# A list scheduler's urgency taken from a backward pass in which every engine does one operation at a time

## The chip, the core and the metric

One core of a Trainium2 chip runs the whole program. The metric is the time of one execution on the device in microseconds (us), the median of three runs. The core has the engines TensorE (PE in the profile), VectorE (DVE), ScalarE (ACT) and GpSimd (POOL); SyncE (SP) issues most of the transfers, ScalarE some.

## The reference

A retention block (attention with a decay in place of the softmax) is followed by a two-layer network with a PReLU between:

```python
# q, k, v: (8, 8, 576, 64) float32
scores = scale * np.matmul(q, k.transpose(0, 1, 3, 2))          # scale = 1/8
gamma = 1.0 - 2.0 ** (-5.0 - np.arange(H))                      # one decay per head
Dmat = np.where(rel >= 0, gamma[:, None, None] ** rel, 0.0)     # rel = row - column
attn = np.matmul(scores * Dmat, v)
x = attn.transpose(0, 2, 1, 3).reshape(4608, 512)
h = x @ w_in                                                    # (512, 2048), float64 input
g = np.maximum(h, 0.0) + alpha * np.minimum(h, 0.0)             # alpha: (2048,)
out = (g @ w_out).astype(np.float32)                            # (2048, 512), float64 input
```

## The kernel before

The sequence of 576 tokens is worked in chunks of 64. A "pair" is two heads of one batch; there are 32 pairs. A "joint" of a pair computes scores inside the chunks, and the state that is carried from chunk to chunk; the masked scores and the states go through small transfers into `at` and `vn`, and the "values" of the pair are computed from them in the next joint. Their results land in tiles `x` of 256 tokens, 18 in all, which the network consumes.

The network's products are made of reduced-precision pieces (`fp32r`) that together keep float32's accuracy: an operand is split into three pieces, and each unit does three products. The first units are done with plain float32 operands instead, while the weights are still being converted (from float64 words, on ACT, DVE and POOL) and split.

Every operation is first recorded in `ops` in program order, with its engine, a cost, and its dependencies (by tile and key), and only then put in order by `plan()` and emitted:

```python
def do(eng, cost, fn, r=(), w=(), late=0.0, lock=False):   # records one operation
    ...
def dma(to, fro, size, r, w, eng="SP"):
    queue = {"SP": nc.sync, "ACT": nc.scalar}[eng]
    do(eng, 0.56, lambda: queue.dma_start(to(), fro()), r, w, late=size / RATE)
```

The operations that are spoken of below, with the line that the profile gives them (cuts marked with "..."):

```python
# L629, L631 (ACT), L639, L641, L650 (DVE), L653 (POOL): one piece of a weight, from float64 words to float32
def convert(raw, wa, to, c=None): ...
# L677 (ACT), L678 (POOL), L681 (DVE): a float32 weight into three pieces
def split_w(at, room_=None): ...

# a pair's operands
def operands(n):
    ...
    do("POOL", 1.15, f, (), four, lock=True)                    # L719: q scaled, qx <- qx, tabx
    ...                                                         # L726: transposes on DVE
    do("ACT", 0.7, f, (), [(kn, 0), (kn, 1)])                   # L731: k scaled, kn <- kn, tabk

def values(n, pv):
    ...  nc.tensor.matmul(pv[i]..., vns[n % 2][:, h2, j], mt.get()[:, h2, j], ...)    # L747, into psh
    ...  nc.scalar.copy(g.get()[:, c, o * C:(o + m) * C], pv[i]...)                   # L762, x <- psh

def joint(n):
    pv = [Gen(psh[m]) for m in range(2)]
    ...  values(n - 1, pv)
    ...                                                         # L785: last chunk's scores, into psh
    ...                                                         # L793: scores, into psa
    ...                                                         # L802: states of the chunks, into psa
    # L816 (ACT) and L822 (POOL), or L831 (DVE): masks; L838 (DVE): the last chunk's
    # L844, L854 (ACT), L849, L857, L860 (DVE): prefix states su, from psa; then stored and loaded as vn

def split_x(vis):        # L906, L918 (ACT), L920, L923 (POOL): x into its three pieces lx
def unit_plain(cell):    # L940 (PE, psh), L946 (ACT), L951 (DVE): first layer, plain
def second_plain(cell):  # L970 (PE, pso): second layer, plain
def unit(cell):          # L1004 (PE, psh), L1012, L1016 (ACT), L1013, L1019 (DVE)
def split_g(cell):       # L1028, L1030 (ACT), L1032, L1035 (POOL)
def second(cell):        # L1053 (PE, pso); L1071, L1076 (DVE): the sums leave PSUM
```

`plan()` is a list scheduler. It walks forward in time; at each step it takes, for every engine, the operations whose dependencies are met, and among those that can start within a small slack of the earliest it picks the one with the smallest `due`. How `due` is made is what changes:

```python
at = 0.0
want = [1e9] * len(ops)
for op in ops:
    if op.eng == "PE":
        want[op.n] = at
        at += op.cost
best = None
for turn in range(TURNS):                    # TURNS = 1
    due = [1e9] * len(ops)
    for op in reversed(ops):
        due[op.n] = min([want[op.n]] + [due[u.n] - wait(op, u) - op.cost - op.late
                                        for u in users[op.n]])
    ...                                      # the forward pass
    while len(order) < len(ops):
        for e, queue in ready.items():
            ...
            c = [(earliest(op), op) for op in queue
                 if e != "PE" or op.n <= rest[0] + AHEAD_PE]
            t0 = min(t for t, _ in c)
            t, op = min((x for x in c if x[0] <= t0 + SLACK.get(e, 0.05)),
                        key=lambda x: (due[x[1].n], x[1].n))
```

Each engine then runs its operations in the order in which they are emitted.

Of the kernel before, what the change touches and what calls it, by code (L numbers as in the profile page):

```python
# [21 lines left out]
def kernel(  # L22
# [95 lines left out]
    for i in range(NBIT - 1):  # L118
# [8 lines left out]
                            op=ALU.mult)  # L127
# [37 lines left out]
    ops = []  # L165
# [56 lines left out]
    LAT = {"PE": 0.2}  # L222

    def plan():

        users = [[] for _ in ops]
        for op in ops:
            for d in op.deps:
                users[d.n].append(op)

        def wait(d, op):
            return 2.0 if d.late else 0.0 if d.eng == op.eng else LAT.get(d.eng, 0.1)

        at = 0.0
        want = [1e9] * len(ops)
        for op in ops:
            if op.eng == "PE":
                want[op.n] = at
                at += op.cost
        best = None  # L240
        for turn in range(TURNS):
            due = [1e9] * len(ops)
            for op in reversed(ops):
                due[op.n] = min([want[op.n]] + [due[u.n] - wait(op, u) - op.cost - op.late
                                                for u in users[op.n]])
            left = [len(op.deps) for op in ops]
            ready = {e: [] for e in BEGIN}
            rest = [op.n for op in ops if op.eng == "PE"]
            end, begin, order = [0.0] * len(ops), [0.0] * len(ops), []
            free, held, port, wire = dict(BEGIN), {}, [0.0, ""], 0.0  # L250
            can = [0.0] * len(ops)
            for op in ops:
                if not op.deps:
                    ready[op.eng].append(op)

            def earliest(op):
                t = max(free[op.eng], can[op.n])
                for b in op.banks:
                    if b in held:
                        t = max(t, max([x + LAT.get(e, 0.1) for e, x in held[b].items()  # L260
                                        if e != op.eng] or [0.0]))
                if op.lock and port[1] != op.eng:
                    t = max(t, port[0])
                if op.late:
                    t = max(t, wire - BACKLOG)
                return t

            while len(order) < len(ops):
                pick = None
                for e, queue in ready.items():  # L270
                    if not queue:
                        continue
                    c = [(earliest(op), op) for op in queue
                         if e != "PE" or op.n <= rest[0] + AHEAD_PE]
                    if not c:
                        continue
                    t0 = min(t for t, _ in c)
                    t, op = min((x for x in c if x[0] <= t0 + SLACK.get(e, 0.05)),
                                key=lambda x: (due[x[1].n], x[1].n))
                    if pick is None or t < pick[0]:  # L280
                        pick = t, op
                t, op = pick
                ready[op.eng].remove(op)
                if op.eng == "PE":
                    rest.remove(op.n)
                begin[op.n] = t
                free[op.eng] = t + op.cost
                end[op.n] = t + op.cost
                if op.late:
                    wire = max(wire, t + op.cost) + op.late  # L290
                    end[op.n] = wire
                for b in op.banks:
                    held.setdefault(b, {})[op.eng] = t + op.cost
                if op.lock:
                    if port[1] == op.eng or t + op.cost > port[0]:
                        port[:] = [t + op.cost, op.eng]
                order.append(op)
                for u in users[op.n]:
                    left[u.n] -= 1
                    can[u.n] = max(can[u.n], end[op.n] + wait(op, u))  # L300
                    if not left[u.n]:
                        ready[u.eng].append(u)
            total = max(end)
            if best is None or total < best[0]:
                best = total, order, begin[:], end[:]
            for op in ops:
                if op.eng == "PE":
                    want[op.n] = 0.5 * want[op.n] + 0.5 * (begin[op.n] - GAIN * (op.n / len(ops)))
        return best

    TURNS, AHEAD_PE, GAIN = 1, 150, 0.0
    BACKLOG = 2.0
    LAG, FIRST = 2, range(4, 8)
    SLACK = {"PE": 0.02}
    BEGIN = {"PE": 5.0, "ACT": 0.5, "DVE": 8.2, "POOL": 5.8, "SP": 0.5}
# [553 lines left out]
    order = [(0, (0, 1)), (1, (0, 1, 2, 3)), (0, (2, 3))]  # L869
# [310 lines left out]
    at = 8  # L1180
# [19 lines left out]
    for cell in cells[8:]:  # L1200
# [6 lines left out]
        for _ in range(late.get(n, 0)):  # L1207
            at = nlate[0]
# [14 lines left out]
    for cell in pend:  # L1223
        second(cell)
    best = plan()
    for op in best[1]:
        op.fn()
# [31 lines left out]
```

## Time and profile before

| | |
|---|---|
| median of 3 runs | 987.82 us (987.67 to 990.02) |
| span of the profiled execution | 988.3 us |
| instructions | 22,760 |
| mean granted TensorE clock | 0.981 of full speed |
| transfers | 134.93 MB, 137 GB/s over the span |
| DMA share of the 16 engines, first 25 us and next 25 us | 1.10 and 1.02 |

The profile is of one execution. Busy time is given for each engine, with the number of instructions; a row of 40 digits shows the busy share in each fortieth of the span (24.7 us), in tenths. The time that is asked about is the time of the last instruction, so what counts is the chain of work that ends there, and the idle time of the engine that carries that chain. A wait is put down to what released it: "PE psh L785 <- ACT x L762" is idle time of PE before line 785 which ended when line 762 on ACT was done. A group shown as "x8" in a timeline is eight instructions drawn together.

### The profile page before, as it was taken

The numbers are of one execution on the slowest core, as the hardware profiler recorded it, in microseconds if no ns is written. First come the engines' busy times: TensorE is split into PE (matmuls) and PEld (weight loads), VectorE is DVE, ScalarE is ACT, GpSimd is POOL, SyncE is SP. The second block draws the span as 40 slices with busy tenths as digits, with TensorE's granted clock in tenths as the row PEclk, the third lists the DMA queues.
The fourth block names the chain that finished last, engine by engine and source line by source line (L and its number), as shares of the span: only waits on it lengthen the run. The fifth ranks groups of instructions, "written<-read, shape, count | busy, mean of one in ns | idle before, by whom it ended". The sixth has DMA issues, their size and how long they took to land.

```text
span 988.3 us, 22760 instructions
## 1 busy us (share of the span) xinstructions
PE 942.5 (95%) x8713; PEld 825.2 (83%) x8713; DVE 614.6 (62%) x1294; ACT 582.9 (59%) x1313; POOL 636.1 (64%) x515
## 2 busy tenths in 40 slices
PE   4897889999999999998999999999999999999998
PEld 4664568898888888887888899999999999999996
DVE  5767766778566777785656777564455444544444
ACT  3564455757566757574677766665555555555542
POOL 3757655666766758575596999675655556566543
PEclk9797989999999999999999999999999999999999
DMA  9969688788665978778442545243222221221111
GB/s 240 211 135 228 145 201 177 184 177 200 171 135 145 209 157 215 169 202 184 152 160 97 162 147 161 74 143 105 64 64 75 71 92 64 65 75 54 43 44 64
DMA packets 255052, 134.93 MB, mean 137 GB/s; under 512 B 218448, under 2 KB 218464, under 8 KB 254944
## 3 DMA queue, kind: packets, MB, share of 16 engines
q1 hardware_dynamic: 238624, 130.59, 51.1%
q10 hardware_dynamic: 16320, 2.89, 2.0%
q8 instruction: 68, 1.11, 0.5%
q14 instruction: 40, 0.33, 0.1%
HBM read 82.19 MB, written 35.65 MB: 119 GB/s over the span
## 4 chain that ended last, share of the span: by engine, by line
PE 82%; DMA 5%; SPq 3%; issue 3%; DVE 2%; POOL 2%; ACT 2%; ACTq 0%; POOLq 0%; DVEq 0%
PE psh L1004 36%; PE pso L1053 35%; PE psh L747 3%; SPq L220 3%; DMA kn<-in_k_dram 2%; PE psh L940 2%; PE pso L970 1%; PE psa L793 1%; PE psa L802 1%; DMA qx<-in_q_dram 1%; DMA w<-in_q_dram 1%; DMA w<-in_moe_w_out_dram 1%; PE psh L785 1%; DMA vn<-in_v_dram 0%; POOL lx L923 0%
## 5 line engine op out<-in xcount | busy, mean ns | idle before, releaser
L1004 PEld LDWEIGHTS psh<-lx,w 128*128 128x128 f32 x3264 | 411.3, 192 | 15.8 <-DVE ga L1019 2.5
L1004 PE MATMUL psh<-lx,w 128*128 128x256 f32 x3264 | 420.5, 285 | 2.3 <-DVE ga L1019 0.9
L1053 PE MATMUL pso<-w,g 128*128 128x512 f32 x1632 | 403.1, 394 | 1.1 <-POOL g L1035 0.7
L1053 PEld LDWEIGHTS pso<-w,g 128*128 128x128 f32 x1632 | 296.9, 189 | 58.9 <-POOL g L1035 1.7
L1032 POOL TENSOR_TENSOR g<-ga,g 128x512 fp32r<-128x512 f32 x136 | 179.2, 1318 | 254.2 <-ACT g L1028 253.9
L1013 DVE SCALAR_TENSOR_TENSOR ga<-psh,gt 128x256 f32<-128x256 f32 x272 | 114.4, 421 | 185.0 <-ACT gt L1012 179.7
L1035 POOL TENSOR_TENSOR g<-g 128x512 fp32r<-128x512 f32 x136 | 177.4, 1304 | 11.6 <-ACT g L1030 1.4
L1019 DVE SCALAR_TENSOR_TENSOR ga<-psh,malpha,ga 128x256 f32<-128x256 f32 x272 | 130.6, 481 | 69.9 <-ACT psh L1016 68.0
L1016 ACT ACTIVATE psh<-ga 128x256 f32<-128x256 f32 x272 | 105.2, 388 | 92.5 <-DVE ga L1013 91.7
L1028 ACT ACTIVATE g<-ga 128x512 fp32r<-128x512 f32 x136 | 85.8, 631 | 116.9 <-PE pso L1053 98.1
L1012 ACT COPY gt<-psh 128x256 f32<-128x256 f32 x272 | 100.9, 371 | 58.2 <-PE psh L1004 50.3
L923 POOL TENSOR_TENSOR lx<-lx 128x512 fp32r<-128x512 f32 x78 | 100.9, 1308 | 17.5 <-DVE lx L913 16.9
L1030 ACT ACTIVATE g<-ga 128x512 fp32r<-128x512 f32 x136 | 84.4, 620 | 0.0
L831 DVE SCALAR_TENSOR_TENSOR at<-psa,pf,mask 64x256 f32<-64x256 f32 x96 | 46.4, 483 | 17.1 <-PE psh L747 9.5
L906 ACT ACTIVATE lx<-x 128x512 fp32r<-128x512 f32 x78 | 47.2, 627 | 0.0
L719 POOL TENSOR_TENSOR qx<-qx,tabx 128x576 f32<-128x576 f32 x28 | 32.6, 1165 | 21.6 <-DMA qx<-in_q_dram 10.4
L747 PEld LDWEIGHTS psh<-at,vn 128*64 128x64 f32 x1008 | 32.9, 137 | 12.9 <-issue 7.6
L920 POOL TENSOR_TENSOR lx<-x,lx 128x512 fp32r<-128x512 f32 x30 | 38.5, 1299 | 3.8 <-ACT lx L918 3.8
L747 PE MATMUL psh<-at,vn 128*64 128x64 f32 x1008 | 38.1, 226 | 2.3 <-DVE ga L1019 2.1
L1071 DVE TENSOR_TENSOR op<-pso,op 128x512 f32<-128x512 f32 x46 | 31.5, 685 | 13.7 <-PE pso L1053 13.7
L731 ACT ACTIVATE kn<-kn,tabk 128x576 f32<-128x576 f32 x28 | 21.7, 776 | 24.4 <-DMA kn<-in_k_dram 22.4
L762 ACT COPY x<-psh 128x256 f32<-128x256 f32 (+3 forms) x84 | 23.8, 320 | 18.7 <-PE psh L747 9.5
(173 smaller groups left out, 868.3 us busy)
## 6 DMA issues: line engine op xcount, KB each, us to landing
ok<-o SPq DMA_DIRECT2D x48, 256.0 KB, 3.4
op<-ok SPq DMA_DIRECT2D x24, 512.0 KB, 4.0
x<-xk SPq DMA_DIRECT2D x23, 512.0 KB, 3.6
xk<-x SPq DMA_DIRECT2D x18, 512.0 KB, 4.2
out_dram<-o SPq DMA_DIRECT2D x36, 256.0 KB, 4.1
kx<-in_k_dram SPq DMA_DIRECT2D x112, 72.0 KB, 3.3
vn<-in_v_dram SPq DMA_DIRECT2D x56, 144.0 KB, 3.5
at<-qT SPq DMA_DIRECT2D x56, 144.0 KB, 3.4
```

What stands on the lines that cost most here:

```text
L747: nc.tensor.matmul(pv[i].get()[half(h2), (j - js[0]) * C:(j - js[0] + 1) * C], vns[n % 2][:, h2, j], mt.get()[:, h2, j], start=True, stop= ...
L923: do("POOL", 1.29, lambda c=c: nc.gpsimd.tensor_tensor(out=piece(to.get()[:, 2, c]), in0=to.get()[:, 0, c], in1=to.get()[:, 1, c], op=ALU. ...
L1004: nc.tensor.matmul(at(b), piece(w[:, l, c0:c0 + P]), piece(x.get()[:, l, cc]), start=(n == 0 and cc == 0), stop=(n > 0 and cc == NCC - 1), ...
L1012: do("ACT", 0.36, lambda t=t, at=at: nc.scalar.copy(t(), at(1)), [(ph, 1)], [(gt, f)])
L1013: do("DVE", 0.42, lambda t=t, g=g, at=at: nc.vector.scalar_tensor_tensor(out=g(), in0=at(0), scalar=ONE, in1=t(), op0=ALU.mult, op1=ALU.su ...
L1016: do("ACT", 0.39, lambda g=g, at=at: nc.scalar.activation(at(1), g(), ACTF.Relu, scale=-1.0), [(ga, f)], [(ph, 1)])
L1019: do("DVE", 0.48, lambda g=g, at=at, fc=fc: nc.vector.scalar_tensor_tensor(out=g(), in0=at(1), scalar=malpha[:, fc:fc + 1], in1=g(), op0=A ...
L1028: do("ACT", 0.64, lambda: nc.scalar.mul(piece(to.get()[:, 2]), ga.get(), BELOW), both, [(to, 2)])
L1030: do("ACT", 0.64, lambda: nc.scalar.mul(piece(to.get()[:, 0]), ga.get(), BELOW * 2.0 ** -12), both, [(to, 0)])
L1032: do("POOL", 1.29, lambda: nc.gpsimd.tensor_tensor(out=piece(to.get()[:, 1]), in0=ga.get(), in1=to.get()[:, 2], op=ALU.subtract), both + [ ...
L1035: do("POOL", 1.29, lambda: nc.gpsimd.tensor_tensor(out=piece(to.get()[:, 2]), in0=to.get()[:, 0], in1=to.get()[:, 1], op=ALU.subtract), [( ...
L1053: nc.tensor.matmul(a[2 * m + b].get(), piece(g.get()[:, l, f, m * P:(m + 1) * P]), piece(w_at[u, 2 + f].get()[:, l]), start=(cell["first"] ...
```

## The change

The order of the operations is to follow better what each engine can do. Before, an operation's urgency was the latest start at which PE could still keep its program order, found along the dependencies alone: many operations of one engine may then be due at once, and the list does not tell which of them has to begin early so that all are done. Now a list scheduler first runs backwards, from the last operation to the first: every engine does one operation at a time, the operation latest in the program goes first, and the time to the end that it finds, negated, is `due`. The loop over `TURNS`, which ran once, is taken out, and with it `want` and `GAIN`. The forward pass, with its costs and constants, is the same:

```diff
-        at = 0.0
-        want = [1e9] * len(ops)
-        for op in ops:
-            if op.eng == "PE":
-                want[op.n] = at
-                at += op.cost
-        best = None
-        for turn in range(TURNS):
-            due = [1e9] * len(ops)
-            for op in reversed(ops):
-                due[op.n] = min([want[op.n]] + [due[u.n] - wait(op, u) - op.cost - op.late
-                                                for u in users[op.n]])
+        due = [0.0] * len(ops)
+        left = [len(users[op.n]) for op in ops]
+        can = [0.0] * len(ops)
+        free = {e: 0.0 for e in BEGIN}
+        ready = {e: [] for e in BEGIN}
+        for op in ops:
+            if not left[op.n]:
+                ready[op.eng].append(op)
+        for _ in ops:
+            pick = None
+            for e, queue in ready.items():
+                if queue:
+                    t0 = min(max(free[e], can[op.n]) for op in queue)
+                    op = max((op for op in queue if max(free[e], can[op.n]) <= t0 + 0.02),
+                             key=lambda op: op.n)
+                    t = max(free[e], can[op.n])
+                    if pick is None or t < pick[0]:
+                        pick = t, op
+            t, op = pick
+            ready[op.eng].remove(op)
+            free[op.eng] = t + op.cost
+            due[op.n] = -(t + op.cost)
+            for d in op.deps:
+                left[d.n] -= 1
+                can[d.n] = max(can[d.n], t + op.cost + wait(d, op) + d.late)
+                if not left[d.n]:
+                    ready[d.eng].append(d)
 ...     (the forward pass: the same, one level further out)
-            for op in ops:
-                if op.eng == "PE":
-                    want[op.n] = 0.5 * want[op.n] + 0.5 * (begin[op.n] - GAIN * (op.n / len(ops)))
-        return best
+        return total, order, begin, end
-    TURNS, AHEAD_PE, GAIN = 1, 150, 0.0
+    AHEAD_PE = 150
```

More of the change, by code (lines that the diff above doesn't have):

```diff
@@ L232, in wait @@
             return 2.0 if d.late else 0.0 if d.eng == op.eng else LAT.get(d.eng, 0.1)
-        at = 0.0
-        want = [1e9] * len(ops)
-        for op in ops:
-            if op.eng == "PE":
-                want[op.n] = at
-                at += op.cost
-        best = None
-        for turn in range(TURNS):
-            due = [1e9] * len(ops)
-            for op in reversed(ops):
-                due[op.n] = min([want[op.n]] + [due[u.n] - wait(op, u) - op.cost - op.late
-                                                for u in users[op.n]])
[L246 to L251, printed above, removed]
-            for op in ops:
[L253 to L279, printed above, removed]
@@ L280, in plan @@
                     if pick is None or t < pick[0]:
                         pick = t, op
-                t, op = pick
-                ready[op.eng].remove(op)
-                if op.eng == "PE":
[L285 to L305, printed above, removed]
@@ L306, in plan @@
-            for op in ops:
-                if op.eng == "PE":
-                    want[op.n] = 0.5 * want[op.n] + 0.5 * (begin[op.n] - GAIN * (op.n / len(ops)))
-        return best
-    TURNS, AHEAD_PE, GAIN = 1, 150, 0.0
+            t, op = pick
[7 more added lines that the diff above has]
+                    ready[d.eng].append(d)
@@ new lines, in plan, with earliest @@
+        left = [len(op.deps) for op in ops]
+        ready = {e: [] for e in BEGIN}
+        rest = [op.n for op in ops if op.eng == "PE"]
+        end, begin, order = [0.0] * len(ops), [0.0] * len(ops), []
+        free, held, port, wire = dict(BEGIN), {}, [0.0, ""], 0.0
+        can = [0.0] * len(ops)
+        for op in ops:
+            if not op.deps:
+                ready[op.eng].append(op)
+        def earliest(op):
+            t = max(free[op.eng], can[op.n])
+            for b in op.banks:
+                if b in held:
+                    t = max(t, max([x + LAT.get(e, 0.1) for e, x in held[b].items()
+                                    if e != op.eng] or [0.0]))
+            if op.lock and port[1] != op.eng:
+                t = max(t, port[0])
+            if op.late:
+                t = max(t, wire - BACKLOG)
+            return t
@@ new lines, in plan @@
+        while len(order) < len(ops):
+            pick = None
+            for e, queue in ready.items():
+                if not queue:
+                    continue
+                c = [(earliest(op), op) for op in queue
+                     if e != "PE" or op.n <= rest[0] + AHEAD_PE]
+                if not c:
+                    continue
+                t0 = min(t for t, _ in c)
+                t, op = min((x for x in c if x[0] <= t0 + SLACK.get(e, 0.05)),
+                            key=lambda x: (due[x[1].n], x[1].n))
+                if pick is None or t < pick[0]:
+                    pick = t, op
+            t, op = pick
+            ready[op.eng].remove(op)
+            if op.eng == "PE":
+                rest.remove(op.n)
+            begin[op.n] = t
+            free[op.eng] = t + op.cost
+            end[op.n] = t + op.cost
+            if op.late:
+                wire = max(wire, t + op.cost) + op.late
+                end[op.n] = wire
+            for b in op.banks:
+                held.setdefault(b, {})[op.eng] = t + op.cost
+            if op.lock:
+                if port[1] == op.eng or t + op.cost > port[0]:
+                    port[:] = [t + op.cost, op.eng]
+            order.append(op)
+            for u in users[op.n]:
+                left[u.n] -= 1
+                can[u.n] = max(can[u.n], end[op.n] + wait(op, u))
+                if not left[u.n]:
+                    ready[u.eng].append(u)
@@ L312 @@
+        total = max(end)
+        return total, order, begin, end
+    AHEAD_PE = 150
     BACKLOG = 2.0
```

## The prediction, made before the changed kernel was run

> **What bounds the kernel now.** I read the mean clock first (0.981 for the core), then section 1 and the slices of section 2, then the table of stretches, then the waits of PE between 80 and 140 us, and last the timelines around the longest of them.
>
> The page says that TensorE is the bound and where it is not yet busy:
>
> ```profile
> PE 942.5 (95%) x8713; PEld 825.2 (83%) x8713; DVE 614.6 (62%) x1294; ACT 582.9 (59%) x1313; POOL 636.1 (64%) x515
> PE   4897889999999999998999999999999999999998
> PEclk9797989999999999999999999999999999999999
> PE 82%; DMA 5%; SPq 3%; issue 3%; DVE 2%; POOL 2%; ACT 2%; ACTq 0%; POOLq 0%; DVEq 0%
> ```
>
> 988.3 - 942.5 leaves 45.8 us in which PE does nothing; that, plus work done at a lowered clock, is all that an order of instructions can win. The stretches (columns: length; busy us and count for PE, PEld, DVE, ACT, POOL; granted clock; DMA share; GB/s) say where it lies:
>
> ```profile
> 0.00:150.00 150.00, 117.36 (x1564) 84.67 (x1565) 102.66 (x219) 74.60 (x149) 91.35 (x93) 0.89 0.88 195
> 150.00:600.00 450.00, 441.73 (x4710) 391.85 (x4709) 319.12 (x691) 294.98 (x692) 316.88 (x246) 1.00 0.67 167
> 600.00:988.30 388.30, 383.43 (x2442) 348.66 (x2440) 192.84 (x386) 213.34 (x473) 227.83 (x177) 1.00 0.25 78
> ```
>
> Idle: 150 - 117.36 = 32.6 us up to 150, 8.3 us from 150 to 600, 4.9 us after. The last are the end: matmuls stop, then two additions, a store and its landing. At the front the clock is 0.89 besides, so some 16 us (150 x 0.11) of clock are lost there, most of it in busy stretches. So the front holds about 49 of the 65 us of loss. There a few waits do most of it (the waits of PE from 80 to 140 us):
>
> ```profile
> PE psh L940 <- POOL g L653: 3.7, 1, 3.7
> PE psh L785 <- ACT x L762: 3.0, 1, 3.0
> PE psh L940 <- ACT x L762: 2.4, 1, 2.4
> PE psa L793 <- ACT kn L731: 2.2, 1, 2.2
> PE psa L793 <- DVE su L857: 1.7, 1, 1.7
> ```
>
> Each line is one single wait (the middle number). That is how a bad order looks, not a slow engine: every time another instruction stands in front of the one that PE needs.
>
> **What the Trainium skill says.** "TensorE: Matmul & The Clock Gate", Part 1, says that an idle array falls to half clock and needs some 3.4 us of sustained work to get back. This trace agrees: eight L940 matmuls at 43.23 took 3.78 us where eight at 60.44 took 1.97, and windows of 3.5 us after the waits show a clock of 0.50. "PSUM — Partial Sum Buffer", Engine vs sequencer instructions, says that ScalarE, VectorE and GpSimd run their queues strictly first in, first out. The trace agrees: POOL stood 7.78 us behind a transfer with other work behind it (shown below). So an order of issue is an order of execution, and one wait at the head stops all behind it.
>
> **The change, part by part.** The program has the same 4,501 planned operations with the same costs, dependencies and tiles: nothing is removed or added. Only "due", the urgency by which the list scheduler picks among ready operations, is made otherwise. Before, PE operations were due at the sum of the PE work ahead of them in program order, and all others from that, backwards through the dependencies alone, as though ten operations of one engine could run at once. Now a backward pass lets each engine do one operation at a time, so a long row of conversions on DVE or POOL begins to count early. Comparing the order in which both programs emit each engine's instructions: 259 of 744 PE operations change place (on average by 0.7 places, at most by 8), 642 of 1,338 on ACT, 647 of 1,253 on DVE, 162 of 500 on POOL, 331 of 666 on SP's queue. The last PE operation that moves follows the 1,524th matmul of L1004, at about 570 us (1,573 have run by 580 us). After it the PE order is the same and PE has no waits worth naming, so what is won or lost before 570 us stays to the end, one for one.
>
> Now the waits, with what the new order does at each.
>
> (a) At 103 us. PE needs the bank psh0, which an ACT copy must empty; in the old order four mask scalings stand before that copy:
>
> ```profile
> 100.74 1.95 ACT L816 ACTIVATE at<-psa,pf 64x256 f32<-64x256 f32 x4 [0.40 <-PE psh L747]
> 102.71 0.49 ACT L762 COPY x<-psh 128x192 f32<-128x192 f32 x2
> 103.08 5.41 PE L940 MATMUL psh<-x,lx 128*128 128x256 f32 x16 [2.39 <-ACT x L762]
> ```
>
> The new order has this copy ahead of the masks. Gain 2.39 us of idle. The 16 matmuls after it took 5.41 us, the same 16 at 120.08 took 3.62: another 1.79 us of lowered clock. Sum 4.2.
>
> (b) At 110.47 us PE waits 1.71 us for psa, which DVE's last step of the prefix states (su, L857) sets free. In the old order five conversion operations (L641, L650, L639, L641, L650, 0.7 us each, 105.57 to 109.2) stand ahead of those steps; in the new one they stand after. The steps come 5 x 0.7 = 3.5 us earlier, and the wait goes. Sum 1.7. The state's store and the values that read it come earlier too.
>
> (c) At 130 to 136 us, before the first units with split operands:
>
> ```profile
> 129.63 1.15 POOL L719 TENSOR_TENSOR qx<-qx,tabx 128x576 f32<-128x576 f32 x1 [7.78 <-DMA qx<-in_q_dram]
> 130.74 2.49 POOL L920 TENSOR_TENSOR lx<-x,lx 128x512 fp32r<-128x512 f32 x2
> 135.75 4.21 PE L1004 MATMUL psh<-lx,w 128*128 128x256 f32 x18 [0.43 <-POOL lx L923]
> ```
>
> POOL's head is a scaling of q (L719) for a pair two joints ahead; it waits for its transfer, and the split of x, ready from ACT at about 128.3 us, stands behind. The new order puts all four split operations before that scaling, and the two joints' states on PE before second layers that can wait. Idle in this stretch: 2.17 + 0.68 + 0.43 = 3.3 us. Lowered clock: 18 matmuls took 4.21 us where 24 take 2.87 elsewhere, so 18 should take 2.15 (2.06 lost), and the six before them took 1.53 for 0.72 (0.81 lost). Sum 3.3 + 2.9 = 6.2.
>
> (d) At 84 to 91 us PE waits 3.0 and then 3.7 us. Behind them is ACT, held from 82 to 83.86 by the keys of the next pair (L731), whose transfer ACT itself issued only at 76.02 and 77.12, after a conversion that waited for weights. The new order issues both ahead of that conversion, at about 74 and 74.6. I take 2 us. The copies that PE needs stay behind the masks, so the rest of this wait stays.
>
> From 0 to 80 us the order of PE, of POOL's first 17 operations and of the weight loads hardly moves, and the 16 DMA engines are full (shares of 1.10 and 1.02 in the first two 25 us): I take 0. From 150 to 600 us there are 8.3 us of idle in pieces under 1.6 us, some of which will go and others come: 0, give or take 3.
>
> Sum: 4.2 + 1.7 + 6.2 + 2.0 = 14.1 us at most. These pieces are not independent: they lie on one chain (states of a pair, store, load back, values, x, split), so what closes one wait brings PE sooner to the next. I count 60% of it, 8.5 us. That share is my choice, not a measurement. 987.8 - 8.5 = 979.3 us, or 0.9%.
>
> **Rivals.** *The front is bound by data, not order.* For it: the DMA shares above, 88% over the first 150 us, and the chain there runs through kn and w transfers of 5.5 to 6.7 us. Against it: the waits in (a) and (b) end with ACT and DVE, behind work that could wait. It would leave 985 to 990 us. *New heads of line.* In strict queues every operation moved ahead may hold others: DVE now has the small alpha operation (L1125, which waits for PE until 22.5 us) before three conversion steps that ran at 19.1 to 21.3. That delays them by 3.7 us; the second half of the first unit, which needs them, now follows a transposition on PE, so I think it is covered. Several such would give 990 to 996 us. *All the lowered-clock stretches go.* If the gaps at the front all fall under what lets the clock drop, up to 16 us come back on top of half the idle: 962 to 968 us. Against it: the gaps of the first 45 us are hardly touched by the new order, and two of the five stretches at half clock (21 to 28 and 42 to 49 us) lie there.
>
> **Range and chances.** Centre 979.3. The first two rivals make the upper end, the third and the full 14 us the lower: 969 to 989 us 8 times in 10. A 2% gain needs 968.1 us or less, so nearly 20 us, a third of all loss: 0.08. A 2% loss needs 1,007.6 us, over 19 us of new waits on a PE that is full from 150 us on: 0.03. Within 2%: 0.89.
>
> **What would show it.** In the new profile, PE's busy time from 150 us on should be as now, and the idle and clock of the first 150 us should carry the difference. (a) is right if L940 no longer waits for L762 with masks before it; (b) if L793 waits for no L857; (c) if POOL L920 begins before the L719 that waits for q, and L1004 begins about 6 us earlier, near 128 us; (d) if the kn transfer is issued near 74 us. The prediction is wrong if L1004 begins as early as that and the end does not follow, which would mean that 150 to 600 us took the gain back, or if new single waits over 2 us appear in the front.

## The result, and the profile after

The changed kernel took 980.36 us (median of 4 runs, 978.37 to 981.99), the kernel before beside it 987.75 us: a ratio of 0.9924, with a 95% interval of 0.9895 to 0.9952. Timed once more later (e9_again below), the ratio came out as 0.9935 (0.991 to 0.996), 6.6 us. So about 7 us are won, 0.7%. The total was foretold within 1.1 us. Where it comes from was not.

Lines of kernel.py after the planner are numbered 11 higher in the changed kernel: L1004 is now L1015, L1053 is L1064, L940 is L951 and L951 is L962, L747 is L758, L762 is L773, L785 is L796, L793 is L804, L802 is L813, L731 is L742, L1019 is L1030. Lines quoted from a kernel have its own numbers.

Section 1 of the page of the changed kernel:

```profile
PE 938.9 (96%) x8713; PEld 822.9 (84%) x8713; DVE 615.4 (63%) x1294; ACT 583.8 (60%) x1313; POOL 638.1 (65%) x515
```

The same three stretches as in the prediction (columns: length; busy us and count for PE, PEld, DVE, ACT, POOL; clock; DMA share; GB/s):

```profile
0.00:150.00 150.00, 117.38 (x1609) 86.00 (x1613) 102.15 (x220) 76.44 (x151) 93.34 (x95) 0.90 0.95 198
150.00:600.00 450.00, 448.05 (x4747) 397.36 (x4738) 324.96 (x700) 300.40 (x704) 324.78 (x251) 1.00 0.68 170
600.00:978.30 378.30, 373.45 (x2375) 339.50 (x2373) 188.25 (x375) 206.95 (x459) 219.96 (x170) 1.00 0.24 76
```

Read the second column. Idle up to 150 us: 150 - 117.38 = 32.6 us, exactly as before. From 150 to 600 us: 1.95 us, where it was 8.3. The front, which was to carry the whole gain, shows none in its idle time; the middle, which was to stay, gave up 6.3 us.

Yet three of the five waits that the prediction listed in the front are gone, a fourth (L785 for L762) is down from 3.0 to 0.9 us, and only the one for POOL's conversion (L653, now L664) has stayed. The two longest waits of PE from 80 to 140 us in the changed kernel tell why that did not help (the others are under 2 us):

```profile
PE psh L758 <- DMA kx<-in_k_dram: 6.8, 1, 6.8
PE psh L951 <- POOL g L664: 3.8, 1, 3.8
```

One new stop of 6.8 us stands at the top. Its timeline, PE first, then what DVE did meanwhile, in two pieces, then SP's queue:

```profile
108.14 2.94 PE L758 MATMUL psh<-at,vn 128*64 128x64 f32 x36 [6.75 <-DMA kx<-in_k_dram]
```

```profile
100.63 0.78 DVE L737 STREAM_TRANSPOSE kT<-kx 128x576 f32<-128x576 f32 x1 [1.98 <-DMA kx<-in_k_dram]
```

```profile
104.24 0.69 DVE L652 TENSOR_SCALAR psa<-psa 128x512 int32<-128x512 int32 x1
104.97 0.69 DVE L661 SCALAR_TENSOR_TENSOR g<-w,psa 128x512 int32<-128x512 int32 x1
105.69 0.69 DVE L650 TENSOR_SCALAR psa<-w 128x512 f32<-128x512 f32 x1
106.42 0.70 DVE L652 TENSOR_SCALAR psa<-psa 128x512 int32<-128x512 int32 x1
107.02 0.86 DVE L962 SCALAR_TENSOR_TENSOR ga<-gt,malpha,psh 128x256 f32<-128x256 f32 x2
```

```profile
103.09 2.18 SPq L220 DMA_DIRECT2D kx<-in_k_dram  x4
105.38 1.15 SPq L220 DMA_DIRECT2D vn<-su  x2
```

The profile names `kx`, but L758 reads only `at` and `vn`, and it writes the bank psh. Two things were missing when PE reached these values early. The bank was one: L962 reads it last, its input from ACT was there at 101.76 us, and DVE came to it only behind a transposition that stood 1.98 us for its keys, the state's arithmetic and four conversion steps in a row; it ended at 107.89 us, and L758 began 0.25 us later. In the kernel before, such conversions stood ahead of the state's arithmetic, which is the wait of (b); the new order moved them behind it, and there they stood ahead of the bank. The other was the states: four loads of `kx` stood ahead of their transfers in SP's line, and the states landed at 108.51 and 109.01 us. The clock fell to 0.52 and 0.51 in the two 3.5 us after 105 us. A new head of line (an operation at the front of an engine's queue that holds all behind it) took the place of the old ones.

To see how time is won along the way, I matched every matmul of two traces to its planned operation and compared the moments at which the same PE work was done. The lead of the changed kernel over the one before, in us (the times in the head are those of the kernel before):

| at | 103 | 150 | 437 | 460 | 480 | 520 | 600 and later |
|---|---|---|---|---|---|---|---|
| first profile | 7.2 | 2.2 | 1.8 | 4.6 | 7.3 | 8.5 | 10.0 |
| a second profile of the same kernel | | 1.2 | -1.5 | 1.4 | 3.4 | 4.6 | 6.1 |

7.2 us were in hand at 103 us and gone again by 108, and another peak of 7.7 near 137 us likewise. The gain that stays is made between 450 and 580 us: 8.3 us in one profile, 7.7 in the other. The profiled execution of the kernel before took 990.23 us, 2.4 more than its median of 987.82, so leads over it come out larger than the gain in medians.

What stood there before? PE in the kernel before, where the last pairs of the attention end:

```profile
456.88 0.33 PE L802 MATMUL psa<-vn,kn 64*64 64x64 f32 x2 [1.57 <-DMA vn<-in_v_dram]
457.94 0.79 PE L802 MATMUL psa<-vn,kn 64*64 64x64 f32 x30 [0.74 <-DMA vn<-in_v_dram]
```

It waits for values `vn`, which SP issues late, behind keys that are needed later and behind the small load `x<-wk`:

```profile
447.17 1.58 SPq L220 DMA_DIRECT2D kx<-in_k_dram  x3
448.79 0.50 SPq L220 DMA_DIRECT2D x<-wk  x1
449.38 1.64 SPq L220 DMA_DIRECT2D kn<-in_k_dram  x2
451.12 1.22 SPq L220 DMA_DIRECT2D at<-qT  x2
452.38 1.35 SPq L220 DMA_DIRECT2D vn<-in_v_dram  x2
```

and ACT stands meanwhile at a scaling of keys that have not landed:

```profile
454.89 0.78 ACT L731 ACTIVATE kn<-kn,tabk 128x576 f32<-128x576 f32 x1 [2.74 <-DMA kn<-in_k_dram]
```

In the changed kernel the same load goes out 4.0 us earlier, while PE is only some 1.8 us ahead there, and the scaling waits 0.45 us (SP's timeline after, then ACT's). The three loads of `kx` no longer stand in between; the keys `kn` and `x<-wk` still go ahead of `vn`, at 444.00 and 445.44 us:

```profile
448.36 1.36 SPq L220 DMA_DIRECT2D vn<-in_v_dram  x2
```

```profile
447.91 0.78 ACT L742 ACTIVATE kn<-kn,tabk 128x576 f32<-128x576 f32 x1 [0.45 <-DMA kn<-in_k_dram]
```

### The profile page after: what moved, and what is told of

It is laid out like the page before. It is cut to its first block, busy times and chain, and to the rows that moved or that the text cites. A ratio compares the mean times of both kernels' runs of the same rounds, so it can differ in the third digit from the quotient of the medians.

```text
span 978.3 us, 22758 instructions
## 1 busy us (share of the span) xinstructions
PE 938.9 (96%) x8713; PEld 822.9 (84%) x8713; DVE 615.4 (63%) x1294; ACT 583.8 (60%) x1313; POOL 638.1 (65%) x515
## 4 chain that ended last, share of the span: by engine, by line
PE 85%; DMA 6%; DVE 3%; POOL 2%; issue 2%; ACT 1%; SPq 1%; ACTq 0%; POOLq 0%; DVEq 0%
PE psh L1015 38%; PE pso L1064 36%; PE psh L758 3%; PE psh L951 2%; DMA kn<-in_k_dram 2%; PE psa L804 1%; PE pso L981 1%; PE psa L813 1%; DMA vn<-su 1%; DMA w<-in_q_dram 1%; SPq L220 1%; DMA kx<-in_k_dram 1%; DMA op<-in_moe_w_in_dram 1%; DMA w<-in_moe_w_out_dram 1%; DVE at L842 0%
## 5 line engine op out<-in xcount | busy, mean ns | idle before, releaser
L1015 PEld LDWEIGHTS psh<-lx,w 128*128 128x128 f32 x3264 | 410.6, 192 | 14.0 <-DVE ga L1030 2.0
L1015 PE MATMUL psh<-lx,w 128*128 128x256 f32 x3264 | 420.0, 284 | 0.4 <-DVE ga L1030 0.3
L1064 PE MATMUL pso<-w,g 128*128 128x512 f32 x1632 | 402.8, 393 | 1.0 <-POOL g L1046 1.0
L1064 PEld LDWEIGHTS pso<-w,g 128*128 128x128 f32 x1632 | 295.8, 188 | 57.9 <-POOL g L1046 2.1
L1030 DVE SCALAR_TENSOR_TENSOR ga<-psh,malpha,ga 128x256 f32<-128x256 f32 x272 | 130.2, 480 | 67.9 <-ACT psh L1027 66.9
L758 PEld LDWEIGHTS psh<-at,vn 128*64 128x64 f32 x1008 | 34.8, 143 | 18.9 <-issue 11.5
L758 PE MATMUL psh<-at,vn 128*64 128x64 f32 x1008 | 39.9, 232 | 9.3 <-DMA kx<-in_k_dram 6.8
L730 POOL TENSOR_TENSOR qx<-qx,tabx 128x576 f32<-128x576 f32 x28 | 32.6, 1166 | 23.9 <-DMA qx<-in_q_dram 17.9
L773 ACT COPY x<-psh 128x256 f32<-128x256 f32 (+3 forms) x84 | 23.7, 321 | 18.2 <-PE psh L758 12.5
L924 DVE TENSOR_TENSOR lx<-x,psa 128x512 fp32r<-128x512 f32 x48 | 32.6, 679 | 2.1 <-PE psh L1015 1.9
```

The costliest lines, as they stand in the source:

```text
L758: nc.tensor.matmul(pv[i].get()[half(h2), (j - js[0]) * C:(j - js[0] + 1) * C], vns[n % 2][:, h2, j], mt.get()[:, h2, j], start=True, stop= ...
L1015: nc.tensor.matmul(at(b), piece(w[:, l, c0:c0 + P]), piece(x.get()[:, l, cc]), start=(n == 0 and cc == 0), stop=(n > 0 and cc == NCC - 1), ...
L1030: do("DVE", 0.48, lambda g=g, at=at, fc=fc: nc.vector.scalar_tensor_tensor(out=g(), in0=at(1), scalar=malpha[:, fc:fc + 1], in1=g(), op0=A ...
L1064: nc.tensor.matmul(a[2 * m + b].get(), piece(g.get()[:, l, f, m * P:(m + 1) * P]), piece(w_at[u, 2 + f].get()[:, l]), start=(cell["first"] ...
```

## The experiments

The first theory after the result: the gain lies at the end of the attention (430 to 610 us) and is made of heads of line that are gone; the front gives nothing. The rival: the front gives the gain, and the single profile hides it. A third possibility: both parts are needed together. The last four experiments ask which property of the new urgency does it. PE's idle time by stage, in us:

| | 0 to 150 | 150 to 430 | 430 to 500 | 500 to 610 | ratio to before |
|---|---|---|---|---|---|
| before | 32.6 | 3.0 | 3.8 | 1.5 | |
| after | 32.6 | 1.2 | 0.8 | 0.0 | 0.9924 |
| e9_again (after) | 34.6 | 2.7 | 1.2 | 0.0 | 0.9935 |
| e1_front | 33.7 | 3.2 | 5.4 | 0.0 | 1.0000 |
| e2_back | 30.3 | 3.2 | 2.5 | 4.9 | 1.0046 |
| e6_sfront | 36.2 | 2.5 | 3.0 | 1.3 | 0.9996 |
| e7_sback | 30.8 | 2.9 | 6.0 | 0.0 | 0.9986 |
| e3_late | 34.8 | 1.0 | 6.0 | 1.5 | 1.0018 |
| e5_two | 31.4 | 2.3 | 2.2 | 1.3 | 0.9968 |
| e8_peonly | 35.1 | 1.1 | 2.5 | 0.0 | 0.9958 |
| e10_nolimit | 30.7 | 3.4 | 2.1 | 3.2 | 0.9993 |
| e4_fix | 33.3 | 1.1 | 1.3 | 0.0 | 0.9915 |
| e12_chainfirst | 33.0 | 7.5 | 1.0 | 0.5 | 1.0068 |
| e11_wait35 | 34.1 | 3.6 | 2.1 | 0.6 | 1.0061 |

### One urgency in front, the other behind

e1_front takes the new urgency for operations recorded before number 1,400 (about 275 us) and the old one beyond; e2_back the other way round. The two scales are joined by the mean difference of PE's operations around the cut:

```diff
+        was_due = old_due()
+        near = [op.n for op in ops if op.eng == "PE" and abs(op.n - CUT) < 150]
+        shift = sum(was_due[n] - due[n] for n in near) / len(near)
+        due = [due[n] + shift if n < CUT else was_due[n] for n in range(len(ops))]
```

> The new urgency for operations recorded before number 1,400 (up to about 275 us), the old one for the rest. If the front of the kernel carries the gain, as predicted, this takes the whole of it: 979 to 981 us. If the later part carries it, as the aligned PE times of both traces say (the changed kernel is 2.2 us ahead at 150 us, 1.8 to 3.4 up to 450 us, and 10.0 after 570 us), it is 984.5 to 986.5 us.

> The old urgency up to number 1,400, the new one for the rest. If the front carries the gain: 986 to 988 us. If the later part carries it: 979.5 to 982 us, and the wait of L802 for vn at 457 us is gone.

e1_front took 987.65 us, ratio 1.0 (0.9985 to 1.0015): the total of the new front with the old urgency behind is that of the kernel before, to within 1.5 us. Its profile has a stop of its own, 2.62 us at 442.94 us. e2_back took 992.49 us, 1.0046 (1.0026 to 1.0065), so the new back alone, made in this way, loses. Its waits of PE from 500 to 610 us show losses that neither parent has (its lines are numbered 28 higher than in the kernel before: L1032 is L1004, L1081 is L1053):

```profile
PE psh L1032 <- DVE ga L1047: 2.6, 4, 1.0
PE pso L1081 <- POOL g L1063: 1.4, 1, 1.4
```

The forward pass compares due times of operations on both sides of the cut, and two scales joined by one shift may not compare well; that this is why it loses was not tested. Exact splices avoid the question.

### Exact splices of the two orders

Both planners run; the emitted order is the first one's up to PE's 353rd operation (about 437 us), then the rest in the other's order. e6_sfront begins with the new order, e7_sback with the old:

```diff
+    for op in first:
+        if op.eng == "PE":
+            count += 1
+            if count > 353:
+                break
+        line.append(op)
+    begun = set(line)
+    line += [op for op in second if op not in begun]
```

> Exact splice: every engine has the changed kernel's order up to PE's 353rd operation (about 437 us), and after it the operations that are left in the order of the kernel before. If the gain lies after 437 us (idle of PE from 430 to 610 us: 5.3 us before, 0.8 us after, with a half-clock stretch more before): 986 to 988 us. If the front carries it: 979 to 981.

> Exact splice the other way: the order of the kernel before up to PE's 353rd operation, the changed kernel's order for what is left. If the gain lies after 437 us: 980 to 983 us. If the front carries it: 987 to 988. If both parts are needed together, neither splice gains.

e6_sfront: 988.13 us, 0.9996 (0.9977 to 1.0016). Again a total without gain. But this splice too has a stop right behind its seam: 1.85 us for POOL at 447.38 us, with the clock at half for 3.4 us from 447.7 us on, so its total alone doesn't clear the rival. (Its profile is of the longest of its executions, 993.64 us.) e7_sback: 986.44 us, 0.9986 (0.9971 to 1.0002), which by its total is a miss for the theory. Its longest wait of PE from 430 to 500 us shows the seam (L891 is L793 of the kernel before, L1114 is L1016):

```profile
PE psa L891 <- ACT psh L1114: 4.8, 1, 4.8
```

That stop, at about 450 us, exists in neither parent; PE's lead drops by 7 us around it. From there to 600 us the spliced kernel gains 8.2 us, as the changed kernel does (8.3). That fits the theory but doesn't show it: after a stop of that length the loads that PE would have waited for have had time to land. A total of a hybrid contains its seam, so these totals leave it open whether the new order behind gains without the new order in front.

### Two heads of line, by hand

e3_late is the kernel before with three issues of SP (the `x<-wk` load and two of `kn`) put behind the `at` and `vn` loads; e5_two moves one more operation, ACT's scaling of `kn` (L731), behind work that is ready:

```diff
+    for some, other in [((2800, 2464, 2465), 2430),    # SP: in e3_late and e5_two
+                        ((2520,), 2486)]:              # ACT: in e5_two alone
+        them = [op for op in line if op.n in some]
+        line = [op for op in line if op.n not in some]
+        at = [op.n for op in line].index(other) + 1
+        line[at:at] = them
```

> The kernel before, with only three transfers moved in SP's queue, all near 450 us: the load of k for the next pair but one (two transfers) and a prefetch of a weight go behind the four transfers that load q and v of the next pair. If that queue order caused the stop at 457 us, L802 loses its two waits of 2.3 us and the half-clock stretch after them: 982 to 984 us. If a full set of 16 DMA engines caused it, the same wait returns elsewhere: 986.5 to 988.5 us.

> The kernel before with the three transfers of e3 moved in SP's queue, and on ACT the scaling of k that stood 6.4 us at the head of the queue in e3 (for a pair two joints ahead) put behind the seven operations of the unit in work. If two heads of line, on SP and on ACT, held the stretch at 450 to 460 us together, both waits go: about 5 us of idle and clock less, 983 to 985 us. If the transfers there are late whatever the order, a third operation stops PE: 987 to 990 us.

e3_late took 990.34 us, 1.0018 (1.0002 to 1.0035): no gain, if anything a loss. PE's wait for `vn` fell from 2.3 to 0.3 us, and a longer one opened 5 us further on. ACT, then PE, in e3_late:

```profile
453.50 0.78 ACT L731 ACTIVATE kn<-kn,tabk 128x576 f32<-128x576 f32 x1 [6.37 <-DMA kn<-in_k_dram]
```

```profile
456.03 2.93 PE L1053 MATMUL pso<-w,g 128*128 128x512 f32 x6 [4.66 <-DVE o L1076]
```

Loading the keys later moved the wait to ACT, which stood 6.37 us at their scaling, with the copies that free PE's banks behind it. With that scaling moved too, e5_two took 985.22 us, 0.9968 (0.9953 to 0.9984): 3.2 us won by four operations out of 4,501, and in its profile the lead over the kernel before grows by 2.8 us from 450 to 460 us, where the stop was. The two queues' heads belong together here; moving SP's alone gained nothing. These are not the moves that the changed kernel makes (there `kn` stays ahead of `vn` and is issued earlier), but the stop that they remove is the same, and it goes without the new front.

### The new stop in the front

e4_fix is the changed kernel with DVE's transposition that waited for `kx` put behind the state's arithmetic, and the four `kx` loads behind the state's transfer.

```diff
+    for some, other in [((455,), 380), ((462, 463, 464, 465), 382)]:   # moved as above
```

> The changed kernel with two moves at 100 us: on DVE one transposition of k for a later pair (it waited 1.98 us for its transfer) goes behind the prefix states of the pair in work, and on SP the four loads of k go behind the two stores of these states. If two heads of line hold the chain of the joints, the wait of 6.75 us at 108 us falls by about 3 us, and the lead holds: 976 to 978.5 us. If what is won there is lost again at the next link (the wait at 137 us): 979.5 to 981 us.

980.74 us, 0.9915 (0.9885 to 0.9945): the same as the changed kernel. The transfers of the states went out from 102.29 us on instead of 105.38, and the last landed at 105.16 us, yet the stop kept its length (the longest wait of PE up to 150 us in e4_fix):

```profile
PE psh L758 <- DVE ga L962: 6.2, 1, 6.2
```

L962 ended at 106.46 us, behind the same four conversion steps, and L758 began at 106.72, again 0.26 us later. So it is the bank behind the conversions that holds PE, an order and not data; moving L962 ahead of them was not tried.

### The changed kernel again

> The changed kernel once more, to see how far a single profile of it scatters and to sharpen the ratio. If the gain lies in the end of the attention work (430 to 610 us) and the front gives nothing: total 979 to 982 us, TensorE idle for at most 2.5 us from 150 to 610 us again (the kernel before: 8.3), and idle in the front within 2 us of 32.6, whichever single stops make it up. If the front carries part of the gain, and the first profile only happened not to show it: idle in the front under 30 us.

983.42 us against 990.03 us for the kernel before beside it, 0.9935 (0.991 to 0.996). The total lies above the expected range; the kernel before, too, took longer than in the first comparison. The stop in the front is there again (8.1 us, ending 0.25 us after L962). PE's idle time from 150 to 610 us was 3.9 us, more than the 2.5 expected and half of the 8.3 before. The two profiles of this one kernel are 3.3 us apart at 437 us (table of leads). So a single profile can't settle a question of 3 us in the front. All of them together say more. The same lead over the kernel before, for the versions with the new order up to 437 us and those with the old one, in us:

| | order up to 437 us | 150 | 437 | 600 |
|---|---|---|---|---|
| after | new | 2.2 | 1.8 | 10.0 |
| e9_again (after) | new | 1.2 | -1.5 | 6.1 |
| e4_fix | new, two moves | 4.1 | 3.5 | 10.8 |
| e6_sfront | new | -2.2 | -4.6 | -3.6 |
| before | old | 0 | 0 | 0 |
| e7_sback | old | 2.0 | 1.5 | 2.8 |
| e3_late | old | 1.6 | 4.5 | 1.6 |
| e5_two | old | 2.1 | 2.5 | 5.9 |

At 437 us the four with the new order lie at -0.2 us on average, the four with the old one at 2.1: the new front is not ahead. From there to 600 us the three runs of the changed kernel gain 7.3 to 8.2 us. So the gain lies behind 437 us; whether all of it could be had without the new front is not shown.

### Which engines the backward pass limits

e8_peonly lets only PE do one operation at a time in the backward pass; e10_nolimit lets no engine be limited, so that urgency is the plain longest path to the end:

```diff
-            free[op.eng] = t + op.cost
+            if op.eng == "PE":                  # e8_peonly; in e10_nolimit both lines are out
+                free[op.eng] = t + op.cost
```

> The changed kernel, but in the backward pass only PE does one operation at a time; DVE, ACT, POOL and the queues do any number. If the limit on every engine is what makes the order good, the gain goes: 986 to 992 us. If the reckoning back from the end with PE in line is enough, it stays: 979 to 982 us.

> The backward pass of the change with the one line left out that keeps an engine busy while it does an operation: urgency is then the plain longest path to the end, with no engine limited. If the gain comes from giving every engine one operation at a time: no gain left, 985 to 990 us, since limiting TensorE alone left half of it (984.95). If it comes from counting back from the end instead of from TensorE's program order, limits aside: 980 to 983 us.

e8_peonly: 984.95 us, 0.9958 (0.994 to 0.9976). e10_nolimit: 990.32 us, 0.9993 (0.9975 to 1.0011). Without any limit, counting back from the end wins nothing in total. With PE alone limited the ratio lies between the two, and the time between the two ranges expected of it. But the intervals of e8_peonly and of the changed kernel (up to 0.9952 and 0.996) overlap: that the other engines' limits add to it is likely, not shown.

A total can hide parts that cancel. The profiled execution of e10_nolimit, the shortest of its twelve (986.01 us), has a clock of 0.97 up to 150 us, where the changed kernel had 0.90, and is 8.9 us ahead of the kernel before at 150 us; its span is only 4.0 us shorter. So without limits the front was better, and the rest lost it. The waits of PE from 430 to 610 us in e10_nolimit (line numbers here are 10 higher than in the kernel before: L1014 is L1004, L1029 is L1019):

```profile
PE psh L1014 <- DVE ga L1029: 5.2, 5, 1.6
```

Five times PE waits for DVE to empty a bank. One of them, 0.98 us, ends at 514.61 us; DVE ahead of it:

```profile
510.76 1.38 DVE L651 TENSOR_SCALAR wa<-wa 128x512 int32<-128x512 int32 x1
512.17 1.66 DVE L660 SCALAR_TENSOR_TENSOR wa<-op,wa 128x512 int32<-128x512 int32 x1
513.75 0.41 DVE L1023 SCALAR_TENSOR_TENSOR ga<-psh,gt 128x256 f32<-128x256 f32 x1
514.09 0.47 DVE L1029 SCALAR_TENSOR_TENSOR ga<-psh,malpha,ga 128x256 f32<-128x256 f32 x1
```

Two conversion steps, 3.04 us together, stand ahead of the two that empty the bank. In the changed kernel the same two steps run near 509 us and take 0.42 and 1.68 us, and PE is idle for 0.0 us from 500 to 610. So what runs beside a step counts too: L651 took 1.38 us with an operation of POOL beside it (510.57 to 511.86 us) where its like, begun while POOL was idle (507.7 to 509.23 us), took 0.42; these are single instances. Which moves of operations spare the changed kernel all five waits was not taken apart.

### The attention's chain first

e12_chainfirst keeps the old urgency and takes 4 us from the due time of every operation of the joints.

```diff
+            due = [due[op.n] - BONUS * op.chain for op in ops]     # BONUS = 4.0
```

> The kernel before, with its old urgency, but with 4 us taken from the due time of every operation of the joints: the attention chain goes first and nothing else changes. If all that the change does is to put the attention's chain ahead of conversions and splits: 979 to 983 us. If what it does is to place each engine's operations so that none stands at the head of a line before its data is there, which moving one chain ahead does not do: 986 to 995 us, with TensorE idle for over 5 us from 150 to 610 us.

993.89 us, 1.0068 (1.0036 to 1.01), with PE idle for 9.0 us from 150 to 610 us. Putting one chain first, at this one bonus, does not do what the change does.

### A longer wait for transfers

e11_wait35 is the changed kernel with the model's wait after a transfer set to 3.5 us, nearer to what the traces show.

```diff
-            return 2.0 if d.late else ...
+            return 3.5 if d.late else ...
```

> The changed kernel with the wait after a transfer set to 3.5 us in the schedule's model, near the 3.4 us that the profiles show as the median from issue to landing, in place of 2.0. If what is left to win are heads of line that wait for transfers which the model believes landed (the 6.8 us stop at 101 us behind the stored states): under 978 us, and the stop under 3 us. If the next link of the attention chain takes it up, as when two moves at that stop were tried (980.74 us): 979 to 983 us. A schedule that differs in 1,800 places on ScalarE may also bring new stops of its own: above 983 us.

995.7 us, 1.0061 (1.0038 to 1.0084): worse than both kernels. The 6.8 us stop did shrink to 1.17 us, but PE stops of 3.88 us (L981, for DVE's L962) at 111 us and 2.77 us (L804, for ACT) at 135 us stand in its place. Moreover PE's busy time is 949.2 us against 938.9 at the same clock (0.983 and 0.984); why its matmuls took longer isn't settled. None of these versions beats the changed kernel. This one also warns of a rival that stands untested: it keeps the limit on every engine, alters one constant, and is 12 us slower than e9_again, timed beside it, so a time belongs to one order as much as to the rule that made it. That a good order fell to this rule by chance could be told only by other kernels or by varied constants under both rules.

## Why the prediction was right in its total and wrong in its place

- **"The front holds about 49 of the 65 us of loss"**: right as a sum, wrong as the place of the gain. Nor do the five waits listed there "do most of it": they sum to 13.0 of 32.6 us, and waits of up to 4.4 us stand before 80 us.
- **(a), (b), (c), (d)**: each local change took place. No L951 waits for L773 behind masks (a); no L804 waits over 0.5 us for the state (b); POOL's four splits run from 124.57 to 129.8 us ahead of the scaling at 129.75, and L1015 begins at 128.56 us, as foretold "near 128" (c); `kn` is issued at 72.10 and 72.77 us (d).
- **"I count 60% of it, 8.5 us"**: this step failed. Its own sign of failure came: "new single waits over 2 us appear in the front". The share that stayed was about 0: at 437 us the kernels with the new front are not ahead of those with the old. What the sum left out is where displaced work goes. In (b) the conversions were to stand after the state's steps; they did, and there they stood ahead of L962, which frees the bank that the values need. The stop there took 6.75 us (6.24 with the transfers moved out of the way) and most of the lead of 7.2 us.
- **"150 to 600 us: 0, give or take 3"**: this failed too, by 6 to 8 us. The idle time there was read as "pieces under 1.6 us", to be won or lost by chance. But the pieces were costlier than their length. Around 457 us two waits summed to 2.3 us, and the clock was 0.70 in the 3.5 us after 457 us and 0.81 in the next, another 1.7 us (3.5 x 0.30 + 3.5 x 0.19). "TensorE: Matmul & The Clock Gate", Part 1, of the Trainium skill puts the fall of the clock after an idle window of about 3.4 us; here waits of 2.3 us in pieces sufficed. Besides, PE is idle for 0.0 us from 500 to 610 us in the changed kernel, so no later wait took the gain back.
- **The sum of the gain after 450 us**: the first profile's 8.3 us are 4.5 of idle time (5.3 to 0.8 from 430 to 610 us) and 1.7 of clock; the other 2.1 lie between matmuls that the trace counts as busy, and are not explained.
- **The rival "new heads of line"** was right for the front, as a loss that about balanced the gain. **The rival "the front is bound by data"** got no support at the one place tried: in e4_fix the transfers came earlier, and an operation of DVE behind conversions held PE as long. For the front as a whole it stays open.
- So two errors of about the same size, +8.5 where there was 0 and 0 where there was 6 to 8, made a right total: that was luck. The range was honest about the sum and says nothing for the reasoning.

On the cause: in this kernel the gain goes when the limit is taken out of the backward pass (e10_nolimit), and comes in part with PE's alone (e8_peonly). That the stop at 457 us, held by heads of two queues, is part of it is shown by e5_two, which removes it by hand and wins 3.2 us. That the rest is of the same kind was not tried move by move, and whether the rule makes good orders elsewhere is not shown.

## What to carry to other kernels

When work is moved out of the way of one wait, ask whose way it stands in next, before counting the wait as won: here conversions moved from ahead of a chain's arithmetic to ahead of the operation that frees its bank, and the lead went there. Small waits in the last stage that still has any may be worth more than large ones in a stage where the next wait is already due. A load and its consumer stood at the heads of two queues, and both had to be moved together; moving the load alone turned a 2.3 us wait into a 4.7 us one. When a list scheduler gets its urgency from dependencies alone, giving each engine one operation at a time in that pass is a cheap thing to try: here it helped, a bonus for a favoured chain on the old urgency did not, nor did a longer wait for transfers on top of the new one.

## What the runs showed of the hardware that was not expected

Two profiled executions of one kernel, with equal orders on every engine, lay 1.0 us apart at 150 us, 3.3 at 437 us and 3.9 at the end, without coming closer again. "PSUM — Partial Sum Buffer", Engine vs sequencer instructions, of the Trainium skill has ScalarE, VectorE and GpSimd run strictly in order; the trace agrees: in e3_late ACT stood 6.37 us before a scaling, and a copy whose matmuls had ended at 448.29 us ran only behind it, at 454.18. SP's queue did the same in effect: in e3_late the `vn` load was issued at 446.27 us, ahead of `x<-wk` and `kn`, and in the kernel before, behind them, at 452.38 us.
